# Attention into a soft mixture of experts: routing computed from the transposed attention weights, without building the attention output

## The chip, the cores and the metric

The kernel runs on one core of a Trainium2 chip. The metric is the device time of one execution in microseconds (us). A core has five engines with queues of their own: PE multiplies matrices into PSUM, DVE (VectorE) and ACT (ScalarE) work on rows of elements, POOL (GpSimd) does too but not on PSUM, and SP issues DMAs. PEld is PE's loading of weights, which overlaps its matmuls.

## What is computed

```
k = v = meanpool_4x4(kv).reshape(B, 768, 128) @ w_sr          # B = 4
a = softmax(q @ k.T / sqrt(128))                              # q: (4, 12288, 128)
x = (a @ v).reshape(49152, 128)                               # attention output
logits = x @ phi                                              # 32 slots
d = softmax(logits, over the tokens); slot_input = d.T @ x    # 32 x 128
slot_out = relu(slot_input @ w1[e]) @ w2[e]                   # 8 experts, 4 slots each
c = softmax(logits, over the slots);  out = c @ slot_out      # (49152, 128)
```

The host only transposes and reorders arrays. The output is 25.17 MB.

## The kernel before

The 49152 queries are cut into 96 blocks of 512 (`NB`), 24 to a batch. Every number is split into a high and a low part (`hi`, `lo`), so that a product of two such numbers is three matmuls (hi hi, hi lo, lo hi).

**A block.** ACT and POOL split the queries (`q_hi`, `q_lo`). `qk` makes scores with the 768 keys on partitions (six tiles) and 512 queries along the row. The maximum over the keys then crosses partitions: `rowmax1` (DVE, a reduction that transposes 32x32 squares), `rowmax2`, `rowmax_pe` (a matmul), `rowmax3`, `rowmax4` (a transpose that spreads the maximum again). `sub` (DVE) takes it off the scores, `exp_hi` and `exp_t` (ACT) compute each exponential twice, once rounded to f16 and once in f32, and `plo` (POOL) subtracts the two. `av_hi` and `av_lo` multiply these weights P with V, next to which a column of ones (the sum) and V phi (32 columns) stand: 161 columns, 72 matmuls a block. `av_evac` (ACT) copies the result to `xl`.

**A group** of four blocks then runs `g0` to `g7a`: it divides by the sum, takes the logits into `LL`, keeps a running maximum over tokens, forms the exponentials `D`, and multiplies them with the attention output in `xl` (`g7m`), adding to `acc`.

**Batches and end.** The next batch's keys are summed by DMAs with addition (`kv_acc`, `kv_fold`) while a batch runs, and turned into K and V by `kv_ops`. `k_max`, `k_sub`, `k_exp` prepare the softmax over slots. After the last block come the expert layers (`t_psi` to `t_slo`) and the output: `c_t`, `o_mm`, `o_ev`, `o_dma`.

**What sets the order.** The code is not run in the order it is written. Class `Plan` takes every step with an engine, a cost, a priority and the buffers it takes (`acq`) and uses, simulates the engines with those costs, and emits each engine's instructions in that order; on the chip the engines follow it, waiting on semaphores. Buffers come in rings, e.g. `m` (two PSUM banks for small results), `t` (f32 exponentials). PSUM's other six banks hold scores.

Of the kernel before, what the change touches and what calls it, by code (L numbers as in the profile page):

```python
# [33 lines left out]
class Plan:  # L34
# [22 lines left out]
    def emit(self):  # L57
# [16 lines left out]
        sums = {key: sum(ops[n][0] == "PE" for n in u) for key, u in self.users.items()}  # L74
        summed = {}
# [4 lines left out]
        tops = [None] * self.cap["m"]  # L80
        where = {}
# [6 lines left out]
        def bank(key):  # L88
            found = []
            for b in range(len(banks)):  # L90
                if key[0] == "pq":
                    t = gone(banks[b])
                    beside = banks[b] is not None and banks[b][1][0] == "px" and t == inf
                    if beside:
                        t = summed.get(banks[b], inf)
                    found.append((max(t, gone(tops[b])), not beside, b))
                else:
                    found.append((max(gone(banks[b]), gone(tops[b])), False, b))
            return min(found)

        def acquire(n, now):
            t = 0.0
            for key in ops[n][6]:
                ring = key[0]
                if ring == "m":
                    t = max(t, bank(key[1])[0])
# [28 lines left out]
        while todo:  # L135
# [10 lines left out]
            for key in acq:  # L146
                if key[0] == "m":
                    b = bank(key[1])[2]
                    (tops if key[1][0] == "pq" else banks)[b] = key
                    where[key] = self.bank = b  # L150
                else:
                    rings.setdefault(key[0], []).append(key)
            for key in acq + ops[n][11]:
                left[key] -= 1
                part[key] = max(part.get(key, 0.0), end)
                if eng == "PE":
                    sums[key] -= 1
                    if sums[key] == 0:
                        summed[key] = end + self.LAG
# [13 lines left out]
def attention_then_soft_moe(ctx: ExitStack, tc: tile.TileContext, qT, kv0, kvT, w_sr, w_srT, phi, w1, w2, outT):  # L173
# [10 lines left out]
    GQ = 2048  # L184
# [25 lines left out]
    gp = es.enter_context(tc.tile_pool(name="gp", bufs=1))  # L210
# [12 lines left out]
    make_identity(nc, ident)  # L223

# [27 lines left out]
    nc.vector.memset(acc, 0.0)  # L252

# [3 lines left out]
    VU = {}  # L257
# [31 lines left out]
    QKP = 5  # L289
    SL = 0.5  # L290


    def kv_load(plan_):
        t = kvp.tile([P, KVC, NK], F32, tag="kv", name="kv_0", bufs=2).rearrange("p a b -> p (a b)")
        o = 0
        for h, e0, n in plan_:
            k0, k1 = KS[h]
            w = k1 - k0
            for c in range(e0, e0 + n, 2):
                s = R2 * k0 + c * w  # L300
# [36 lines left out]
    PK_ = {}  # L337

    def kv_k_mm(b, h):
# [5 lines left out]
        pk = PK_[b, h] = mt([P, 512], f"pk_{b}_{h}")  # L345
# [3 lines left out]
    def kv_k_hi(b, h):  # L349
        k0, k1 = KS[h]  # L350
        nc.scalar.activation(kT[b][0][:, k0:k1], PK_[b, h][:, : k1 - k0], AF.Copy, scale=1.0 / R2)

    def kv_k_lo(b, h):
# [3 lines left out]
            out=lo[:, k0:k1], in0=PK_.pop((b, h))[:, : k1 - k0], scalar=1.0 / R2, in1=hi[:, k0:k1].bitcast(F32),  # L357
# [12 lines left out]
    def kv_v_out(b, h):  # L370
        nc.scalar.activation(VU[b][:, 3 * h : 3 * h + 3, :], PK_.pop((b, h, "v")), AF.Copy, scale=1.0 / R2)

    def kv_m(b, k, h):
        if k == 0 and h == 0:
            AM[b] = (
                bp.tile([P, 2, 2], F32, tag="am", name=f"am_{b}", bufs=1),
                bp.tile([P, 2, P], F32, tag="dg", name=f"dg_{b}", bufs=1),
                bp.tile([P, 2], F32, tag="am2", name=f"am2_{b}", bufs=1),
# [3 lines left out]
            out=am[:, k, h : h + 1], in_=VU[b][:, 3 * h : 3 * h + 3, VSRC[k]], axis=XY, op=ALU.max,  # L382
            apply_absolute_value=True,
        )
        if h and k:
            nc.vector.tensor_reduce(out=am2, in_=am, axis=X, op=ALU.max)

    def kv_d(b, k):
        _, dg, am2 = AM[b]
        nc.scalar.activation(dg[:, k, :], ident, AF.Copy, scale=am2[:, k : k + 1])  # L390

    def kv_s_mm(b):
        pa = PK_[b] = mt([P, 512], f"pa_{b}")
        nc.tensor.matmul(
            pa[:, : 2 * P], ones, AM.pop(b)[1].rearrange("p k n -> p (k n)"), start=True, stop=True
        )

    def kv_s_g(b):
        pa = PK_.pop(b)
        pg = pa[:, 2 * P : 2 * P + 2]  # L400
        nc.vector.tensor_reduce(out=pg, in_=pa[:, : 2 * P].rearrange("p (k n) -> p k n", k=2), axis=X, op=ALU.max)
        nc.vector.tensor_scalar_max(pg, pg, 1e-30)
        nc.vector.tensor_single_scalar(pg.bitcast(U32), pg.bitcast(U32), 0x7F800000, op=ALU.bitwise_and)
        g = bp.tile([P, 2], F32, tag="g", name=f"g_{b}")
        nc.vector.tensor_scalar_mul(g, pg, 1.0 / VK)
        inv = bp.tile([P, 2], F32, tag="inv", name=f"inv_{b}")
# [3 lines left out]
    VSRC = (slice(0, C), slice(C, C + NS))  # L410

    def kv_t_hi(b, k):
        inv = VS[b][1]
        if k == 0:
            VU[b] = (
                VU[b],
                bp.tile([P, NT, VW], F16, tag="vhi", name=f"vhi_{b}"),
                bp.tile([P, NT, C + NS], F16, tag="vlo", name=f"vlo_{b}"),
            )
        v, hi, lo = VU[b]  # L420
        src = VSRC[k]
        part = hi[:, :, src.start + 1 : src.stop + 1]
        if b:
            nc.scalar.activation(v[:, :, src], v[:, :, src], AF.Copy, scale=inv[:, k : k + 1])
            nc.scalar.activation(part, v[:, :, src], AF.Copy)
        else:
            nc.scalar.activation(part, v[:, :, src], AF.Copy, scale=inv[:, k : k + 1])

    def kv_t_lo(b, k):
        inv = VS[b][1]  # L430
        v, hi, lo = VU[b]
        src = VSRC[k]
        if b:
            if k == 0:
                nc.gpsimd.memset(hi[:, :, :1], 1.0)
            nc.gpsimd.tensor_tensor(out=lo[:, :, src], in0=v[:, :, src], in1=hi[:, :, src.start + 1 : src.stop + 1], op=ALU.subtract)
            return
        if k == 0:
            nc.vector.memset(hi[:, :, :1], 1.0)
        nc.vector.scalar_tensor_tensor(  # L440
            out=lo[:, :, src], in0=v[:, :, src], scalar=inv[:, k : k + 1], in1=hi[:, :, src.start + 1 : src.stop + 1],
            op0=ALU.mult, op1=ALU.subtract,
        )


    def q_load(g, lo=0, hi=GQ):
# [3 lines left out]
        eng = nc.scalar if hi < GQ else nc.sync  # L450
        eng.dma_start(out=qs[g][:, lo:hi], in_=qT[b, :, o * GQ + lo : o * GQ + hi])
# [801 lines left out]
```

## Time and profile before

| | |
|---|---|
| median of 3 runs | 1116.59 us (1116.41 to 1117.16) |
| span of the profiled execution, first to last instruction | 1112.9 us |
| mean granted PE clock | 0.976 |
| busy PE / PEld / DVE / ACT / POOL | 1044.9 / 893.6 / 984.2 / 829.4 / 870.5 us |
| DMA | 89.15 MB, mean 80 GB/s |

The profile is of one execution, and its own time is given as the span; what lies around the span isn't profiled, and the runs' median is 3.7 us longer. A group row reads: line, engine, operation, output<-input, shapes, count | busy us, mean ns of one | idle time before it and what ended it. A wait row reads: who waited, for whom, us in total, times, longest. A DMA row ends with KB each and us to landing.

### The profile page before, as it was taken

What the parts mean: (1) busy time and instruction counts of PE and PEld (TensorE: products, weight loads), DVE (VectorE), ACT (ScalarE), POOL (GpSimd) and SP (SyncE); (2) the same over time, 40 slices, a digit from 0 to 9 for tenths busy, and PEclk for the clock granted to TensorE, in tenths of its full rate; (3) what the DMA queues carried; (4) which work ended last, traced back from release to release, by engine and by line L of the source; (5) the groups of instructions that cost most, each with busy time, mean ns of one, the idle gap of its engine ahead of it and who ended that gap; (6) DMA issues with size and microseconds to landing.
All of it is one profiled execution on the core that took longest, in us unless ns stands there. A gap on an engine that the chain in (4) does not pass through costs nothing.

```text
span 1112.9 us, 24732 instructions
## 1 busy us (share of the span) xinstructions
PE 1044.9 (94%) x10198; PEld 893.6 (80%) x10198; DVE 984.2 (88%) x1493; ACT 829.4 (75%) x1029; POOL 870.5 (78%) x503
## 2 busy tenths in 40 slices
PE   3699999999999999999999999999999999997885
PEld 2588888888888888888888888888888888886343
DVE  7889889899889989899888988989989988997894
ACT  1677778778777878778777788688778777875563
POOL 0679898798899889789899989789889889873440
PEclk9899999999999999999999999999999999999975
DMA  9218301111136310120145310120110110113498
GB/s 351 108 31 177 70 16 39 39 58 39 39 60 150 82 35 6 39 87 10 39 102 108 82 39 1 39 95 2 39 39 1 39 39 2 39 39 114 145 406 357
DMA packets 17407, 89.15 MB, mean 80 GB/s; under 512 B 1680, under 2 KB 3984, under 8 KB 11152
## 3 DMA queue, kind: packets, MB, share of 16 engines
q1 hardware_dynamic: 13408, 69.47, 17.0%
q0 software_dynamic: 3312, 17.70, 8.4%
q8 instruction: 81, 1.33, 0.5%
q10 hardware_dynamic: 576, 0.41, 0.1%
q14 instruction: 30, 0.25, 0.1%
HBM read 58.87 MB, written 25.17 MB: 76 GB/s over the span
## 4 chain that ended last, share of the span: by engine, by line
PE 61%; ACT 18%; DVE 15%; issue 3%; POOL 2%; DMA 1%; SPq 0%; DVEq 0%; ACTq 0%
PE m L562 10%; PE m L554 10%; PE m L555 9%; ACT phi L528 8%; PE s L476 8%; PE s L478 7%; PE s L477 7%; ACT t L532 7%; DVE t L521 4%; PE m L503 3%; DVE r L483 3%; PE m L707 2%; PE po L1138 2%; DVE o L1147 2%; DVE mb L513 1%
## 5 line engine op out<-in xcount | busy, mean ns | idle before, releaser
L537 POOL TENSOR_TENSOR plo<-t,phi 128x1536 f16<-128x1536 f32 x190 | 598.8, 3156 | 128.1 <-ACT t L532 127.3
L528 ACT ACTIVATE phi<-t,lnk 128x1536 f16<-128x1536 f32 x192 | 301.5, 1570 | 118.9 <-DVE t L521 118.7
L483 DVE TRANSPOSE_TENSOR_REDUCE r<-s 128x32 f32<-128x1024 f32 x288 | 348.6, 1233 | 29.3 <-PE s L478 25.7
L554 PE MATMUL m<-vhi,phi 128*128 128x161 f16 x2280 | 354.7, 234 | 2.8 <-DVE acc L713 1.4
L555 PE MATMUL m<-vlo,phi 128*128 128x160 f16 x2280 | 353.8, 233 | 0.0
L521 DVE TENSOR_TENSOR t<-s,mb 128x1024 f32<-128x1024 f32 (+1 forms) x384 | 342.8, 949 | 9.3
L532 ACT ACTIVATE t<-t,lnk 128x1536 f32<-128x1536 f32 x192 | 301.5, 1570 | 3.6
L476 PE MATMUL s<-qhi,khi 128*128 128x512 f32 x576 | 239.9, 417 | 6.1 <-DVE t L521 5.8
L554 PEld LDWEIGHTS <-phi 128*128 128x128 f16 x2304 | 224.3, 98 | 24.3 <-issue 24.3
L555 PEld LDWEIGHTS <-phi 128*128 128x128 f16 x2304 | 225.1, 98 | 5.4 <-issue 3.5
L562 PE MATMUL m<-vhi,plo 128*128 128x161 f16 x2280 | 226.5, 234 | 0.4 <-POOL plo L537 0.4
L478 PE MATMUL s<-qhi,klo 128*128 128x512 f32 x576 | 226.6, 393 | 0.0
L477 PE MATMUL s<-qlo,khi 128*128 128x512 f32 x576 | 226.1, 392 | 0.0
L562 PEld LDWEIGHTS <-plo 128*128 128x128 f16 x2304 | 178.2, 100 | 1.2 <-POOL plo L537 0.6
L466 POOL TENSOR_TENSOR qlo<-q,qhi 128x512 fp32r<-128x512 f32 x96 | 128.6, 1340 | 26.8 <-ACT qhi L462 26.8
L572 ACT ACTIVATE xl<-m 128x322 f32<-128x322 f32 x189 | 81.4, 430 | 84.5 <-PE m L562 83.8
L476 PEld LDWEIGHTS s<-qhi,khi 128*128 128x128 f32 x576 | 109.2, 190 | 32.6 <-issue 7.5
L478 PEld LDWEIGHTS s<-qhi,klo 128*128 128x128 f32 x576 | 108.8, 189 | 24.7 <-DVE klo L356 0.5
L477 PEld LDWEIGHTS s<-qlo,khi 128*128 128x128 f32 x576 | 109.5, 190 | 18.7 <-issue 0.7
L513 DVE STREAM_TRANSPOSE mb<-m 128x512 f32<-128x512 f32 x96 | 68.3, 711 | 3.3
L462 ACT ACTIVATE qhi<-q 128x512 fp32r<-128x512 f32 x96 | 59.1, 616 | 1.5 <-issue 0.8
L508 DVE TENSOR_REDUCE m<-m 128x16 f32<-128x64 f32 x96 | 21.5, 224 | 40.7 <-PE m L503 40.7
(145 smaller groups left out, 860.1 us busy)
## 6 DMA issues: line engine op xcount, KB each, us to landing
q<-qT SPq DMA_DIRECT2D x23, 1024.0 KB, 4.8
outT<-o SPq DMA_DIRECT2D x21, 1024.0 KB, 5.4
kva<-kvT POOLq DMA_DIRECT2D x9, 1536.0 KB, 11.2
kva<-kvT SPq DMA_DIRECT2D x3, 1536.0 KB, 10.5
kv<-kv SPq DMA_DIRECT2D x8, 512.0 KB, 5.6
w<-w SPq DMA_DIRECT2D x2, 1536.0 KB, 6.4
w<-w SPq DMA_DIRECT2D x4, 768.0 KB, 4.4
outT<-o SPq DMA_DIRECT2D x6, 512.0 KB, 4.7
```

The costliest lines, as they stand in the source:

```text
L466: nc.gpsimd.tensor_tensor(out=lo, in0=q_src(i), in1=hi.bitcast(F32), op=ALU.subtract)
L476: nc.tensor.matmul(s, khi[:, ks], hi, start=True, stop=False)
L477: nc.tensor.matmul(s, khi[:, ks], lo, start=False, stop=False)
L478: nc.tensor.matmul(s, klo[:, ks], hi, start=False, stop=True)
L483: nc.vector.tensor_reduce(out=MX[i][:, 2 * u : 2 * u + 2, :].rearrange("p t b -> p (t b)"), in_=S[i, u].rearrange("p t (b j) -> p (t b) j" ...
L521: nc.vector.tensor_tensor(out=TT_[i, h][:, o : o + n, :], in0=S[i, t // 2][:, u : u + n, :], in1=MX[i].unsqueeze(1).broadcast_to([P, n, BQ ...
L528: nc.scalar.activation(hi, TT_[i, h], AF.Exp, bias=lnk, scale=SCALE)
L532: nc.scalar.activation(t, t, AF.Exp, bias=lnk, scale=SCALE)
L537: eng.tensor_tensor(out=lo, in0=TT_.pop((i, h)), in1=PP[i, h], op=ALU.subtract)
L554: nc.tensor.matmul(px, p, vhi[:, t, :], start=(t == 0), stop=False)
L555: nc.tensor.matmul(px[:, 1:], p, vlo[:, t, :], start=False, stop=False)
L562: nc.tensor.matmul(px, PP[i, t // TH][1][:, t % TH, ks], vhi[:, t, :], start=False, stop=(t == NT - 1))
```

## The change

Scores are made the other way round: queries on partitions (four tiles of 128), the 768 keys along the row. The row's maximum is then a plain reduction (`rowmin`; the keys carry the factor -1/sqrt(128), so that it is a minimum), it enters the exponential as ACT's bias, and ACT adds up the row's sum as it goes (`exp_t`). Each exponential is computed once; ACT copies it to f16 (`t_hi`) and POOL subtracts (`t_lo`).

The attention output is no longer built. The logits are P (V phi): for that P has to stand with keys on partitions. All high tiles and two of six low ones are transposed by DMA (`x_hi`, `x_lo`), the other low ones on PE (`tr`) and copied out by DVE (`tr_out`). `l_mm` then makes the 32 logits of 512 queries, 32 weight columns at a time, in four column strips of PE. Three small transposes turn the 128x128 result back and forth: `l_r` divides by the sum, `colmax` and `d_exp` keep the running maximum and exponentials over tokens, now block by block. The slot inputs are D^T P V: `z_mm` multiplies D with the untransposed P of the block, `z_acc` adds to a 128x768 sum per batch, and only at a batch's end `b_t`, `b_out` and `b_mm` multiply this with V. `f_q` to `f_acc` bring the strips to one maximum at the end.

Around that: the six score banks are two slots of three banks, half a block each; `nh` and `nl` (f16 P) have four buffers, the transposed `pth` and `ptl` two, `t` six of half the size; the q loads move from SP's queue to ACT's and are halved to 512 KB; the sums of keys have one buffer instead of two; three of eight experts' `w1` are loaded early instead of six; the output goes in chunks of three tiles instead of four, through eight buffers instead of four. `Plan` loses its special rule for a bank shared by two results, and its priorities change (`PER`).

```diff
-        nc.tensor.matmul(s, khi[:, ks], hi, start=True, stop=False)
-        nc.tensor.matmul(s, khi[:, ks], lo, start=False, stop=False)
-        nc.tensor.matmul(s, klo[:, ks], hi, start=False, stop=True)
+        cuts = (0, 512, NK) if j % NP == 0 else (0, NK - 512, NK)
+        parts = list(zip(cuts, cuts[1:]))
+        for n, (a, k) in enumerate(((hi, khi), (hi, klo), (lo, khi))):
+            for c0, c1 in parts:
+                nc.tensor.matmul(s[:, c0:c1], a[:, qt], k[:, c0:c1], start=(n == 0), stop=(n == 2))
+
+    def rowmin(i, h):
+        z = (NP * i + h) % NR
+        o = SLOT[i, h] * SW
         nc.vector.tensor_reduce(
+            out=low[:, z, :, 0], in_=sflat[:, o : o + SW].rearrange("p (j k) -> p j k", j=NP), axis=X, op=ALU.min
         )
+        nc.vector.tensor_reduce(out=nm[:, z, :], in_=low[:, z], axis=X, op=ALU.add)
+    def exp_t(i, j):
+        nc.scalar.activation(
+            t, s_of(i, j), AF.Exp, bias=nm[:, z, j % NP : j % NP + 1], scale=-1.0, accum_out=sums[:, i % NR, j, :1]
         )
-        nc.scalar.activation(hi, TT_[i, h], AF.Exp, bias=lnk, scale=SCALE)
-        nc.scalar.activation(t, t, AF.Exp, bias=lnk, scale=SCALE)
+        nc.scalar.activation(nat(NH[i], j), T[i, j].rearrange("p (t k) -> p t k", t=NT), AF.Copy)
+            out=nat(NL[i], j), in0=T.pop((i, j)).rearrange("p (t k) -> p t k", t=NT), in1=nat(NH[i], j), op=ALU.subtract
+    def x_hi(i, h):
+        nc.sync.dma_start_transpose(out=wide(PTH[i], h, 0, NT), in_=run(NH[i], h, 0, NT))
+    def x_lo(i, h):
+        nc.sync.dma_start_transpose(out=wide(PTL[i], h, 0, XT), in_=run(NL[i], h, 0, XT))
...
+        for t in range(XT, NT):
+            for j in range(NP):
+                nc.tensor.transpose(out=b[:, n * P : (n + 1) * P], in_=NL[i][:, h, t, j, :], identity=ident_h)
+        nc.vector.tensor_copy(run(PTL[i], h, XT, NT), b[:, : (NT - XT) * NP * P])
-            nc.tensor.matmul(px, p, vhi[:, t, :], start=(t == 0), stop=False)
-            nc.tensor.matmul(px[:, 1:], p, vlo[:, t, :], start=False, stop=False)
+        for x, u in ((hi, uhi), (hi, ulo), (lo, uhi)):
+            for t in range(NT):
+                for j in range(TB):
+                    nc.tensor.matmul(
+                        pl[j * NS : (j + 1) * NS, :], u[:, t, :], nat(x, j)[:, t, :],
+                        start=(n == 0), stop=(n == 3 * NT - 1),
+                    )
...
+    def z_mm(i, u):
+        for n, (d, x) in enumerate(((0, NH[i]), (1, NH[i]), (0, NL[i]))):
+            for j in range(TB):
+                nc.tensor.matmul(
+                    pz[j * NS : (j + 1) * NS, :], dh[:, d, j * NS : (j + 1) * NS], nat(x, j)[:, u * ht : (u + 1) * ht, :],
+                    start=(n == 0), stop=(n == 2),
+                )
+    def z_acc(i, u):
+            nc.vector.scalar_tensor_tensor(
+                out=z, in0=z, scalar=al[:, i % NRR : i % NRR + 1], in1=pz, op0=ALU.mult, op1=ALU.add
+            )
```

**On PE**, in the middle of the program: `s` and `s6` are score banks, `m0` and `m1` the small banks. Before, the end of a block's scores and the first matmuls of an earlier block's P times V:

```order
L476 MATMUL s_45_2_6464<-qhi_45_6208,khi_1_2403 128x512
L477 MATMUL s_45_2_6464<-qlo_45_6209,khi_1_2403 128x512
L478 MATMUL s_45_2_6464<-qhi_45_6208,klo_1_2404 128x512
L554 LDWEIGHTS phi_43_0_6279
L554 MATMUL m1_115<-vhi_1_3204,phi_43_0_6279 128x161
L555 LDWEIGHTS phi_43_0_6279
L555 MATMUL m1_115<-vlo_1_3205,phi_43_0_6279 128x160
```

Now, the scores of one query tile, a small transpose and the first logit matmul of block 40:

```order
L454 MATMUL s6_120<-khi_1_3432,qhi_44_7951 128x512
L454 MATMUL s6_120<-khi_1_3432,qhi_44_7951 128x256
L454 MATMUL s6_120<-klo_1_3433,qhi_44_7951 128x512
L454 MATMUL s6_120<-klo_1_3433,qhi_44_7951 128x256
L454 MATMUL s6_120<-khi_1_3432,qlo_44_7952 128x512
L454 MATMUL s6_120<-khi_1_3432,qlo_44_7952 128x256
L539 MATMUL m1_119<-ident_84,dt_39_8214 128x128
L527 LDWEIGHTS uhi_1_4456
L527 MATMUL m0_118<-pth_40_7902,uhi_1_4456 32x128
```

A 768-wide row takes two matmuls where there was one of 512, and the 161-wide products with V have given way to 32x128 ones with V phi, four blocks behind the scores.

**On ACT**, a stretch before (`phi` is the f16 exponential, `xl` the copied attention output):

```order
L528 ACTIVATE phi_51_0_7441<-t_51_0_7399,lnk_96 128x1536
L532 ACTIVATE t_51_0_7399<-t_51_0_7399,lnk_96 128x1536
L682 ACTIVATE D_11_7447<-D_11_7447 128x512
L684 ACTIVATE da_11_7449<-da_11_7449 128x32
L528 ACTIVATE phi_51_1_7486<-t_51_1_7438,lnk_96 128x1536
L462 ACTIVATE qhi_54_7507<-q_13_6573 128x512
L532 ACTIVATE t_51_1_7438<-t_51_1_7438,lnk_96 128x1536
L572 ACTIVATE xl_12_7253<-m1_115 128x322
```

and now (`lt` is the logits' copy, `dh` the high part of D):

```order
L467 ACTIVATE t_46_0_8618,sums_110<-s6_120,nm_109 128x768
L467 ACTIVATE t_46_1_8696,sums_110<-s6_120,nm_109 128x768
L535 ACTIVATE lt_42_8702<-m1_119,g_1_4440 128x128
L582 ACTIVATE dh_41_8707<-dr_41_8693 128x128
L418 DMA q_25_8710<-qT 128x1024
L365 ACTIVATE v32_2_8411<-m0_118 128x480
L429 ACTIVATE qhi_48_8735<-q_24_8317 128x512
L383 ACTIVATE dg_2_8506<-ident_84,am2_2_8507 128x128
L482 ACTIVATE nh_45_8762<-t_45_0_8503 128x6x128
L482 ACTIVATE nh_45_8762<-t_45_1_8538 128x6x128
```

The exponentials of a block (46) run a block ahead of its high parts (45 here), and the logits that arrive (42) belong to high parts two blocks further back: those of 43 and 44 lie between.

**On SP**, which held the q loads before:

```order
L755 DMA w1_0_11015<-w1 128x3x1024
L451 DMA q_13_6573<-qT 128x2048
L451 DMA q_14_7157<-qT 128x2048
L451 DMA q_15_7731<-qT 128x2048
L451 DMA q_16_8308<-qT 128x2048
```

and now, two blocks' transposes, each half block a high and a low one:

```order
L502 DMA_TRANSPOSE pth_71_14005<-nh_71_13877 128x12x128
L505 DMA_TRANSPOSE ptl_71_14006<-nl_71_13890 128x4x128
L502 DMA_TRANSPOSE pth_71_14005<-nh_71_13877 128x12x128
L505 DMA_TRANSPOSE ptl_71_14006<-nl_71_13890 128x4x128
L502 DMA_TRANSPOSE pth_72_14162<-nh_72_14037 128x12x128
```

One load a group has become four transposes a block.

More of the change, by code (lines that the diff above doesn't have):

```diff
@@ L86, in gone, with bank @@
             return 0.0 if key is None else freed.get(key, inf)
[L88 to L99, printed above, removed]
+        def bank():
+            return min((gone(key), b) for b, key in enumerate(banks))
         def acquire(n, now):
@@ L575, in bc, with l_sb, t_mm, ll @@
+    def l_sb(i):
+        lt = W["lt", i] = sp.tile([P, P], F32, tag="lt", name=f"lt_{i}")
+        nc.scalar.activation(lt, PK_.pop(("l", i)), AF.Copy, scale=VS[i // BPB][0])
+    def t_mm(key, src):
+        b = PK_[key] = mt()[:, :P]
+        nc.tensor.transpose(out=b, in_=src, identity=ident)
     def bc(a, n):
         return a.unsqueeze(2).broadcast_to([P, a.shape[1], n])
+    def ll(i):
+        return LL[:, i * TB : (i + 1) * TB, :]
+    def l_r(i):
+        nc.vector.tensor_tensor(
+            out=ll(i), in0=PK_.pop(("l1", i)).rearrange("p (j s) -> p j s", j=TB), in1=bc(rr[:, i % NRR], NS), op=ALU.mult
+        )
@@ new lines, in z_acc, with b_t @@
+    def z_acc(i, u):
+        b, ib = divmod(i, BPB)
+        if ib == 0 and u == 0:
+            ZA[b] = sp.tile([P, NK], F32, tag="za", name=f"za_{b}")
+        z = ZA[b][:, u * HK : (u + 1) * HK]
+        pz = PK_.pop(("z", i, u))
+        if ib:
+            nc.vector.scalar_tensor_tensor(
+                out=z, in0=z, scalar=al[:, i % NRR : i % NRR + 1], in1=pz, op0=ALU.mult, op1=ALU.add
+            )
+        else:
+            nc.vector.tensor_copy(z, pz)
+    def b_t(b, u):
+        n = 4 if u == 0 else NT - 4
+        pz = PK_["bt", b, u] = mt()
+        for k in range(n):
+            t = 4 * u + k
+            nc.tensor.transpose(out=pz[:, k * P : (k + 1) * P], in_=ZA[b][:, t * P : (t + 1) * P], identity=ident)
@@ L776, in act @@
         return n / 1200 + 0.08 + 0.093 * aps
-    last = {}
     LAND = 1.46
@@ new lines, in attention_then_soft_moe @@
+        for j in range(TB):
+            h, j2 = divmod(j, NP)
+            p = T0 + 0.25 * PER * j
+            e1 = ops["e", i, j] = op("ACT", act(NK, 1) + ACCT, 0.1, p - 2, [nz[i, h]], lambda i=i, j=j: exp_t(i, j), acq=[("t", (i, j))], use=[("s", (i, h))])
+            e2 = ops["hi", i, j] = op(
+                "ACT", act(NK), 0.1, p + 1, [e1] + ([ops["hi", i, j - 1]] if j else []), lambda i=i, j=j: t_hi(i, j), acq=[] if j else [("nh", i)], use=[("t", (i, j))] + ([("nh", i)] if j else []), raw=0.13
+            )
+            ops["lo", i, j] = op(
+                "DVE" if end else "POOL", 0.9 if end else 1.6, 0.1, p + 2, [e2] + ([ops["lo", i, j - 1]] if j else []), lambda i=i, j=j: t_lo(i, j), acq=[] if j else [("nl", i)],
+                use=[("t", (i, j)), ("nh", i)] + ([("nl", i)] if j else []),
+            )
@@ new lines, in attention_then_soft_moe @@
+        p = T0 + DP * PER
+        u = ("u", b)
+        k = ("m", ("l", i))
+        a = op("PE", 18 * LMM + 0.15, 0.3, p, xs + [ops["u", b]], lambda i=i: l_mm(i), acq=[k], use=[ph, pl, u])
+        a = op("ACT", act(P, 1), 0.1, p, [a], lambda i=i: l_sb(i), acq=[("lt", i)], use=[k])
+        k = ("m", ("l1", i))
+        a = op("PE", 0.13, 0.3, p, [a], lambda i=i: t_mm(("l1", i), W.pop(("lt", i))), acq=[k], use=[("lt", i)])
+        a = ops["L", i] = op("DVE", dve(P) + 0.03, 0.08, p, [a, rc], lambda i=i: l_r(i), use=[k])
@@ new lines, in attention_then_soft_moe @@
+        k = ("m", ("l2", i))
+        a = ops["l2", i] = op("PE", 0.13, 0.3, p, [a], lambda i=i: t_mm(("l2", i), ll(i)), acq=[k])
+        a = op("DVE", 0.3, 0.08, p, [a] + ([nz["nb", i - 1]] if i else []), lambda i=i: colmax(i), use=[k])
+        nz["nb", i] = a
+        de = a = op("ACT", 0.6, 0.1, p, [a], lambda i=i: d_exp(i), acq=[("dt", i)], use=[k])
+        nz["sum"] = op("POOL", 0.2, 0.1, p, [a] + ([nz["sum"]] if i else []), lambda i=i: d_sum(i))
+        k = ("m", ("d", i))
+        a = op("PE", 0.13, 0.3, p, [a], lambda i=i: t_mm(("d", i), W.pop(("dt", i))), acq=[k], use=[("dt", i)])
@@ new lines, in attention_then_soft_moe @@
+        a = op("DVE", dve(P) + 0.03, 0.08, p, [a], lambda i=i: d_r(i), acq=[("dr", i)], use=[k])
+        a = op("ACT", act(P), 0.1, p, [a], lambda i=i: d_hi(i), acq=[("dh", i)], use=[("dr", i)])
+        a = op("POOL", 0.33, 0.1, p, [a], lambda i=i: d_lo(i), use=[("dr", i), ("dh", i)])
+        for v in range(2):
+            k = ("m", ("z", i, v))
+            z = op("PE", 3 * 0.17 + 0.15, 0.3, p, [a], lambda i=i, v=v: z_mm(i, v), acq=[k], use=[("dh", i), nh, nl])
+            za = ("za", b)
+            new = ib == 0 and v == 0
+            prev_acc[v] = op(
+                "DVE", dve(HK) + 0.06, 0.08, p, [z] + ([prev_acc[0] if ib == 0 and v else prev_acc[v]] if i or v else []),
+                lambda i=i, v=v: z_acc(i, v), acq=[za] if new else [], use=[k] + ([] if new else [za]),
+            )
```

886 lines of the change are left out of this document (352 added, 534 removed).

## The prediction

> **What bounds the kernel now.** I read the span and clock first, then busy time in a steady window, then the spacing of blocks, then the chain of waits, and last single groups. One block is 512 queries; there are 96. The window's columns are busy us of PE, PEld, DVE, ACT and POOL, the granted clock, the DMA share and GB/s.
>
> ```profile
> core 0: 1112.9 us, clock 0.976
> core 0: us, PE busy (x) PEld busy (x) DVE busy (x) ACT busy (x) POOL busy (x), PEclk, DMA share, GB/s
> 400.00:600.00 200.00, 197.17 (x1976) 173.28 (x1974) 180.90 (x271) 158.27 (x195) 171.31 (x97) 1.00 0.22 56
> 1090.00:1113.00 23.00, 12.48 (x96) 7.11 (x92) 10.27 (x11) 8.41 (x11) 0.00 (x0) 0.57 0.86 355
> L513 DVE STREAM_TRANSPOSE mb<-m x96: 711/711/714, 30.9 to 1004.6; 128x512 f32<-128x512 f32 x96
> PE 61%; ACT 18%; DVE 15%; issue 3%; POOL 2%; DMA 1%; SPq 0%; DVEq 0%; ACTq 0%
> POOL plo L537 <- ACT t L532: 127.3, 98, 6.9
> ACT phi L528 <- DVE t L521: 118.7, 71, 3.1
> ```
>
> L513 runs once a block: (1004.6 - 30.9)/95 = 10.25 us a block. Of that PE is busy 98.6% (197.17 of 200), so 10.1 us; DVE 9.3, POOL 8.8, ACT 8.1. The chain of waits says the same: 61% of it is PE. ACT and POOL do wait, for each other and for DVE (the two wait lines, about 1.3 us a block each), but PE has no room to let them use it. So the loop is PE-bound at full clock, and 95 x 10.25 = 974 us of the span is loop. The last stretch is output: DMA 86% busy while the engines idle.
>
> **What goes and comes on PE, a block.** Rows that price it, the first four as first and last of seven and of twelve matmuls in a run:
>
> ```profile
> 508.27 0.39 PE L476 MATMUL s<-qhi,khi 128*128 128x512 f32 x1
> 509.63 0.39 PE L476 MATMUL s<-qhi,khi 128*128 128x512 f32 x1
> 506.01 0.23 PE L554 MATMUL m<-vhi,phi 128*128 128x161 f16 x1
> 506.78 0.23 PE L555 MATMUL m<-vlo,phi 128*128 128x160 f16 x1
> L562 PEld LDWEIGHTS <-plo 128*128 128x128 f16 x2304 | 178.2, 100 | 1.2 <-POOL plo L537 0.6 <-issue 0.4
> 1003.82 0.30 PEld L503 LDWEIGHTS m<-rq,sel 128*128 128x128 f32 x2 [0.23 <-DVE rq L495]
> 114.54 1.09 PE L707 MATMUL m<-xl,D 128*32 128x129 f32 x32
> L1058 PE MATMUL ph<-w,sm 128*32 128x512 f32 x32 | 5.0, 782 | 0.3 <-DVE sm L1043 0.3
> L1116 PE MATMUL m<-ident,LL 128*128 128x128 f32 x96 | 18.8, 328 | 3.8 <-POOL LL L747 3.1 <-DVE clo L1126 0.6
> ```
>
> A 512-wide score matmul takes 1.36/6 = 0.227 us, an attention matmul 0.77/11 = 0.070. Removed: 18 x 0.227 = 4.1 us of scores, 48 x 0.070 + 24 x 0.077 (178.2/2304) = 5.2 us of P times V, and the row-maximum and slot matmuls, together the rest of the 10.1. Added:
>
> - Scores: 12 of 512 columns, 2.72 us, and 12 of 256. A 256-wide one is at least half of 0.227; its f32 weight load is the question. Two L503 loads take 0.30 us where one takes 0.19, so they follow each other 0.11 apart: I take 0.115, 1.38 us. If the full 0.19 showed each time it would be 2.28. Scores 4.1 (to 5.0), no gain.
> - 16 f16 transposes of lo tiles at 0.077: 1.24.
> - 72 logit matmuls with 32 weight columns. L707 is the same 128x32 shape, 32 in 1.09 us, 0.034 each; an f32 matmul is two such instructions, an f16 one is one, with half the passes, so 0.017 to 0.034 and 1.2 to 2.45 us. I take 1.5, nearer the low end, since f16 is what runs.
> - 24 slot matmuls of 384 columns on the same tiling. L1058 gives 0.156 for 512 f32 columns; three quarters of it, halved for f16 or not: 0.059 to 0.117, 1.4 to 2.8. I take 1.4.
> - Three small f32 transposes at 0.196 (18.8/96): 0.6. Per-batch work: 0.2.
>
> PE after: 4.1 + 1.24 + 1.5 + 1.4 + 0.6 + 0.2 = 9.0 us, from 8.7 to 12.3.
>
> **ACT.** The four exponentials of 768 read PSUM and take a bias pointer and a sum.
>
> ```profile
> L424 ACT ACTIVATE v<-v,inv 128x768 f32<-128x768 f32 x3 | 2.8, 919 | 0.0
> L425 ACT ACTIVATE vhi<-v 128x768 f16<-128x768 f32 x3 | 2.5, 849 | 0.1
> L462 ACT ACTIVATE qhi<-q 128x512 fp32r<-128x512 f32 x96 | 59.1, 616 | 1.5 <-issue 0.8 <-DMA q<-qT 0.7
> L1104 ACT ACTIVATE shi<-psq,tsum 128x128 fp32r<-128x128 f32 x1 | 0.4, 367 | 0.6 <-PE psq L1099 0.6
> L588 ACT ACTIVATE cq<-quad,cmt 128x4 f32<-128x4 f32 x24 | 6.8, 284 | 1.0 <-DVE cmt L633 1.0
> 500.33 1.56 ACT L528 ACTIVATE phi<-t,lnk 128x1536 f16<-128x1536 f32 x1
> 501.79 0.29 ACT L588 ACTIVATE ru<-r,g 128x16 f32<-128x16 f32 x1
> ```
>
> L424 is a 768-wide operation with a pointer: 0.92. The running sum is in no row; it costs between nothing and another small operation (0.28), and I add 0.1. So exp_t 4 x 1.02, t_hi 4 x 0.85 (L425 is exactly its shape), q_hi 0.62, l_sb 0.37, the two exponentials of d_exp 0.28 + 0.47, d_hi 0.3: 9.5 us of durations. A next operation starts 0.10 before the last has ended (500.33 + 1.56 against 501.79), so 13 of them occupy 8.2. The routing exponentials, per-batch work and the q loads, which now issue from ACT's queue, add about 0.6: 8.8 us (8.4 to 9.5), against 8.1. ACT, which had two us to spare, has none.
>
> **POOL and DVE.**
>
> ```profile
> L537 POOL TENSOR_TENSOR plo<-t,phi 128x1536 f16<-128x1536 f32 x190 | 598.8, 3156 | 128.1 <-ACT t L532 127.3
> L436 POOL TENSOR_TENSOR vlo<-v,vhi 128x768 f16<-128x768 f32 x3 | 4.8, 1591 | 0.0
> L466 POOL TENSOR_TENSOR qlo<-q,qhi 128x512 fp32r<-128x512 f32 x96 | 128.6, 1340 | 26.8 <-ACT qhi L462 26.8
> L747 POOL TENSOR_TENSOR LL<-LL,RM 128x128 f32<-128x128 f32 x1 | 0.4, 402 | 0.0
> L483 DVE TRANSPOSE_TENSOR_REDUCE r<-s 128x32 f32<-128x1024 f32 x288 | 348.6, 1233 | 29.3 <-PE s L478 25.7
> L1147 DVE COPY o<-po 128x1024 f32<-128x1024 f32 x23 | 28.0, 1215 | 5.0 <-PE po L1138 4.9
> L1107 DVE SCALAR_TENSOR_TENSOR slo<-psq,tsum,shi 128x128 fp32r<-128x128 f32 x1 | 0.3, 342 | 0.0
> L695 DVE TENSOR_REDUCE al<-da 128x1 f32<-128x32 f32 x24 | 4.2, 175 | 0.8 <-POOL da L690 0.8
> ```
>
> POOL keeps the big subtraction, cut in four: 4 x 1.59 = 6.36 against 2 x 3.16, plus q_lo 1.34, d_lo 0.4 (L747), d_sum 0.2, and 0.5 for the routing subtraction and DMA issue: 8.8, unchanged; the group arithmetic it loses is made up. On DVE the maximum no longer needs transposes, the cross-partition matmul or the 4 subtractions: two reductions of 1536 (1.5 x 1.23 each as a ceiling, 3.7), z_acc twice 0.6 (between L1107 and L1147 by width), l_r and d_r 0.7, six small ones 1.05, two 1024-wide f16 copies out of PSUM at 0.6 to 1.2 each (half of L1147, or all of it), 0.2 of routing: 8.0 to 9.2, against 9.3. The Trainium skill, VectorE: DVE Perf Modes, "Why PSUM operands drop a tier", lets 16-bit PSUM data run at twice the f32 rate; by that the copies are at the low end and DVE near 8.1, by the row 9.2, and no run here shows it.
>
> **SP and DMA.** Per block 32 tiles of 128x128 f16, 1 MB, now go SBUF to SBUF through DMA transposes, four in a row on SP's queue; no trace of before shows one.
>
> ```profile
> q1 hardware_dynamic: 13408, 69.47, 17.0%
> kva<-kva POOLq DMA_DIRECT2D x3, 768.0 KB, 7.2
> kva<-kva POOLq DMA_DIRECT2D x3, 384.0 KB, 3.9
> L1151 SPq DMA_DIRECT2D outT<-o x27: 332/332/1336, 1045.6 to 1107.1; - x27
> ```
>
> At the plain rate (69.47 MB in 17.0% of 1112.9 us, 367 GB/s) it is 2.9 us. The nearest row is the fold, SBUF to SBUF with an addition: 384 KB more for 3.3 us more, 8.8 us a MB. The addition reads a second operand, so I take half of it, 4.4 us, beside 2.3 us of other traffic (share 0.22). That is hidden under a 9 us block: in the instruction order the high parts and the logits of one block lie two blocks apart, and four nh buffers carry it. If that cover goes, every us over the block length costs 95. Behind SP's waits for these high and low parts stand only each batch's first key load and the expert weights, both issued many blocks or a chain of small steps ahead of use; the q loads have left that queue.
>
> **The sum.** Four engines between 8.0 and 9.2 replace one at 10.1 with the rest below 9.3. The old loop lost 0.15 to waits over its bound; with PE, ACT and POOL within 0.3 of each other a late one has nothing to catch up with, and I allow 0.4, a third of the 1.3 us that POOL alone waits for ACT today: 9.4 us a block. 95 x (9.4 - 10.25) = -81. The end: output is bound by DMA as before (from 1045.6 to the end, 25 MB in 67 us), but about six t_hi are still queued behind the last exponentials, 6 x 0.85 = 5 us (0 to 12; a gain isn't seen, since the rate of the output is the queue's). Head: no change, since the first loads are the same bytes. Span 1112.9 - 81 + 5 = 1037. The runs' median, 1116.6, lies 3.7 above the profiled span, so 1041 us.
>
> **Rivals.** Waits vanish, and the block comes down to its busiest engine, 8.9: 1112.9 - 95 x 1.35 + 8.7 = 993. For it: the old loop ran at 98.6% of its bound. Against: it had one bound, not three.
>
> The lock between ACT and POOL: the t ring has six tiles, so an exponential waits for the low part of six tiles earlier on POOL, which waits for a high part on ACT. Today's two wait lines are this kind; should they keep their 1.2 us, a block is 8.8 + 1.2 = 10.0: 1098.
>
> The transposes bound the loop (slower). If the queue serves them one at a time at the fold's landing times, 2 x (3.9 + 1.7) = 11.2 us, past 10.25; with half of the other traffic in their way 12.4: 1112.9 + 95 x 2.15 + 8.7 = 1326. It decides from 10.25 us a block. Against it: the queue's rows show several transfers in flight. The Trainium skill bears on it from both sides: VectorE: DVE Perf Modes, "The three transpose paths", gives a 128x128 DMA transpose 1309 ns against 390 on TensorE and sends such tiles to TensorE; 32 in series would be an estimated 42 us a block. The same skill's DMA: Bandwidth & Descriptors, "Latency and other measured facts", gives transposes 261 GB/s, by which 1 MB takes an estimated 4.0 us and is hidden. No run here shows either.
>
> PE at its upper end (12.3), with the column tiles not side by side: about 1316. L707 and L1058 speak against it. That the edits do nothing at all needs gains and losses that cancel.
>
> **How the numbers follow.** Forecast 0.50, with 9.1 to 9.7 us a block, 1012 to 1069; waits vanish 0.18; lock 0.17; transposes 0.09; PE 0.03; cancelled 0.03. Slower is the transposes, PE and the worst of the lock (0.03): 0.15; same, within 0.2%, which is about what these timings can tell, 0.03; faster 0.82. The range leaves out the slow rivals (0.13) and the lower third of the fast one (0.06): 985 to 1112.
>
> **What would show it.** rowmin twice a block, spaced 9.4 us a pair; PE busy near 96%, its 128x32 matmuls 0.02 apart; exp_t near 1.0 us and ACT above 90%; transposes landing within a few us. I am wrong if the chain runs through SP or DMA, if ACT's waits for POOL exceed 1 us a block, or if a 256-wide score matmul takes 0.19.

## The result, and the profile after

The changed kernel takes **1664.08 us** (median of 4 runs, 1654.54 to 1670.55) against 1116.88 us before: ratio 1.490, 95% interval 1.485 to 1.495. The forecast was 1041 us, faster. (Where a kernel's times scatter, its median below is of all its runs and its ratio to before only of those near its fastest; x1's ratio alone is of all four.)

After, a steady window, the row minimum (L459, twice a block), the main waits, and the one wait of PE for a transpose. The window's columns are as in the prediction; a wait's are us in total, times and the longest:

```profile
core 0: 1668.8 us, clock 0.823
1000.00:1200.00 200.00, 139.87 (x1830) 104.82 (x1829) 101.04 (x197) 116.53 (x249) 114.71 (x95) 0.86 0.51 97
L459 DVE TENSOR_REDUCE low<-s x192: 1747/1758/1759, 33.2 to 1499.7; 128x2 f32<-128x1536 f32 x192
ACT t L467 <- PE s L454: 282.5, 137, 5.6
PEld s L454 <- ACT t L467: 254.2, 175, 4.2
POOL nl L487 <- ACT nh L482: 246.6, 121, 6.4
DVE low L459 <- ACT t L467: 210.3, 77, 7.3
PE s L454 <- ACT t L467: 204.3, 141, 3.9
ACT t L467 <- DVE low L459: 163.4, 81, 3.9
DVE low L459 <- PE s L454: 154.2, 80, 5.8
PE m L527 <- DMA pth<-nh: 9.5, 1, 9.5
```

A block takes (1499.7 - 33.2)/95.5 = 15.36 us; 9.4 was forecast. No engine is the bound: PE is busy 70% of the window, the others 50 to 58%. PE, DVE and ACT wait for each other in a ring, always over `s`. One of those waits makes no sense as a flow of data: the minimum L459 waits 210 us for the exponential L467, which writes nothing that the minimum reads. PE waits for a transposing transfer once.

Each engine's work on the tile `s` alone (PE, PEld, DVE, ACT) in earlier windows, after and then before:

```profile
200.00:400.00 200.00, 80.38 (x324) 58.45 (x323) 47.44 (x27) 52.68 (x108) 0.86 0.50 100
400.00:600.00 200.00, 78.28 (x318) 55.95 (x317) 47.45 (x27) 51.48 (x105) 0.89 0.69 115
```

```profile
200.00:400.00 200.00, 87.11 (x352) 63.64 (x350) 138.34 (x135) 1.00 0.26 65
```

After, scores, minimum and exponential sum to 80.4 + 47.4 + 52.7 = 180.5 of 200 us. Before, the sum is 87.1 + 138.3 = 225 of 200: they overlapped. By the start and end of each instruction in the trace, no two of these engines work on `s` at once anywhere between 200 and 1000 us. In order of time, PE's, DVE's and ACT's lines on `s` for block 49, up to the first of block 50 (the exponentials at 774.05 and 774.93 are still block 48's):

```profile
771.63 1.76 DVE L459 TENSOR_REDUCE low<-s 128x2 f32<-128x1536 f32 x1 [0.17 <-PE s L454]
...
774.05 0.88 ACT L467 ACTIVATE t<-s,nm 128x768 f32<-128x768 f32 x1
774.93 0.89 ACT L467 ACTIVATE t<-s,nm 128x768 f32<-128x768 f32 x1
...
776.06 0.61 PE L454 MATMUL s<-khi,qhi 128*128 128x512 f32 x2
776.86 0.51 PE L454 MATMUL s<-khi,qlo 128*128 128x512 f32 x2
...
777.49 0.90 ACT L467 ACTIVATE t<-s,nm 128x768 f32<-128x768 f32 x1 [1.32 <-PE s L454]
...
778.53 0.62 PE L454 MATMUL s<-khi,qhi 128*128 128x256 f32 x2 [0.30 <-ACT t L467]
779.33 0.51 PE L454 MATMUL s<-khi,qlo 128*128 128x256 f32 x2
...
779.96 0.90 ACT L467 ACTIVATE t<-s,nm 128x768 f32<-128x768 f32 x1 [0.75 <-PE m L539]
...
780.99 1.76 DVE L459 TENSOR_REDUCE low<-s 128x2 f32<-128x1536 f32 x1 [2.08 <-ACT t L467]
...
782.80 0.80 PE L454 MATMUL s<-khi,qhi 128*128 128x512 f32 x1 [2.40 <-DVE low L459]
```

The scores at 776.06 and 778.53 fill the second slot while the exponentials at 777.49 and 779.96 read the first, so nothing but the tile's name joins them; yet each starts where the other ends. In the program both slots are views of one tile, `s6`, and the order is as if each instruction on any part of that tile waited for all earlier ones of other engines. Before there were three tiles `s0` to `s2`.

### The profile page after: what moved, and what is told of

Its sections match the earlier page's. It is cut to its first block, busy times and chain, and to the rows that moved or that the text cites. A ratio compares the mean times of both kernels' runs of the same rounds, so it can differ in the third digit from the quotient of the medians.

```text
span 1668.8 us, 34763 instructions
## 1 busy us (share of the span) xinstructions
PE 1126.4 (67%) x14062; PEld 823.4 (49%) x14062; DVE 819.7 (49%) x1574; ACT 890.0 (53%) x1890; POOL 882.4 (53%) x748
## 5 line engine op out<-in xcount | busy, mean ns | idle before, releaser
L487 POOL TENSOR_TENSOR nl<-t,nh 128x768 f16<-128x768 f32 x384 | 626.2, 1648 | 247.1 <-ACT nh L482 246.6
L467 ACT ACTIVATE t<-s,nm 128x768 f32<-128x768 f32 x384 | 344.5, 898 | 523.2 <-PE s L454 282.5
L459 DVE TENSOR_REDUCE low<-s 128x2 f32<-128x1536 f32 x192 | 337.4, 1757 | 405.7 <-ACT t L467 210.3
L454 PE MATMUL s<-khi,qhi 128*128 128x512 f32 (+1 forms) x768 | 273.8, 443 | 334.0 <-ACT t L467 204.3
L454 PEld LDWEIGHTS s<-khi,qhi 128*128 128x128 f32 x768 | 138.8, 224 | 420.6 <-ACT t L467 254.2
L482 ACT ACTIVATE nh<-t 128x768 f16<-128x768 f32 x384 | 308.1, 834 | 55.1 <-PE m L596 51.3
L454 PE MATMUL s<-klo,qhi 128*128 128x512 f32 (+1 forms) x768 | 233.7, 391 | 0.0
L454 PE MATMUL s<-khi,qlo 128*128 128x512 f32 (+1 forms) x768 | 233.6, 391 | 0.0
L454 PEld LDWEIGHTS s<-klo,qhi 128*128 128x128 f32 x768 | 160.3, 230 | 22.6
L454 PEld LDWEIGHTS s<-khi,qlo 128*128 128x128 f32 x768 | 160.3, 230 | 22.3
L512 PE MATMUL m<-ident_h,nl 128*128 128x128 f16 x1536 | 135.2, 242 | 33.2 <-DVE dr L575 23.3
L467 ACT ACTIVATION_READ_ACCUMULATOR t<-s,nm 128x1 f32 x384 | 74.9, 195 | 0.0
```

The lines of the kernel that those rows point to most:

```text
L454: nc.tensor.matmul(s[:, c0:c1], a[:, qt], k[:, c0:c1], start=(n == 0), stop=(n == 2))
L459: nc.vector.tensor_reduce(out=low[:, z, :, 0], in_=sflat[:, o : o + SW].rearrange("p (j k) -> p j k", j=NP), axis=X, op=ALU.min)
L467: nc.scalar.activation(t, s_of(i, j), AF.Exp, bias=nm[:, z, j % NP : j % NP + 1], scale=-1.0, accum_out=sums[:, i % NR, j, :1])
L482: nc.scalar.activation(nat(NH[i], j), T[i, j].rearrange("p (t k) -> p t k", t=NT), AF.Copy)
L487: nc.gpsimd.tensor_tensor(out=nat(NL[i], j), in0=T.pop((i, j)).rearrange("p (t k) -> p t k", t=NT), in1=nat(NH[i], j), op=ALU.subtract)
L512: nc.tensor.transpose(out=b[:, n * P : (n + 1) * P], in_=NL[i][:, h, t, j, :], identity=ident_h)
```

## Experiments

Theory A: `s6` as one tile serialises scores, minimum and exponential. Theory B: the transposing transfers and their rings set the period. Theory C: PE is slow because its granted clock fell to 0.82.

**x1: two tiles.** The two slots become two tiles of three banks. Each engine's order in the loop stays; the output stage at the end gets two pairs of banks in place of three.

```
-    s6 = ps.tile([P, 6, 512], F32, tag="s6", name="s6")
+    s3 = [ps.tile([P, 3, 512], F32, tag=f"s{k}", name=f"s{k}") for k in range(2)]
...
-        return sflat[:, o : o + NK]
+        return sflat[SLOT[i, j // NP]][:, o : o + NK]
```

> The one PSUM tile s of six banks becomes two tiles of three banks, one for each pair of query tiles; the order of the loop's instructions stays. Theory A (one tile s is one unit of the semaphores: scores, row minimum and exponential of either half wait for each other, since the rows of tile s fill 177 to 183 of each 200 us and their sum is their union): a block falls from 15.4 us to what its busiest engine needs, 9.2 to 11.5 us by the busy rows of PE, ACT and POOL, so 1100 to 1290 us in all. Theory B (the transposing transfers and the rings of nh and pth set the period): no change, 1640 to 1680 us. Theory C (PE is slow because its granted clock is 0.85): no change either, 1640 to 1680 us.

Measured 1181.37 us median of four (1156.01 to 1196.58; the trace is of the fastest), 1.058 of before (1.054 to 1.063). The minimum's row by line, its wait for the exponential, and a window of the work on `s` (columns as above):

```profile
DVE low L458 <- ACT t L466: 0.8, 2, 0.6
L458 DVE TENSOR_REDUCE low<-s x192: 1726/1757/1761, 36.7 to 1015.4; 128x2 f32<-128x1536 f32 x192
```

```profile
600.00:800.00 200.00, 98.78 (x462) 72.74 (x462) 66.74 (x38) 73.83 (x152) 0.98 0.92 156
```

And four lines in order of time:

```profile
607.19 0.60 PE L454 MATMUL s<-khi,qhi 128*128 128x512 f32 x2
607.60 0.90 ACT L466 ACTIVATE t<-s,nm 128x768 f32<-128x768 f32 x1
607.63 0.51 PE L454 MATMUL s<-klo,qhi 128*128 128x512 f32 x2
607.98 0.52 PE L454 MATMUL s<-khi,qlo 128*128 128x512 f32 x2
```

Now 239 of 200 us; the exponential at 607.60 runs inside the scores of 607.19 to 608.5, and the minimum's wait for the exponential, 210 us before, is down to 0.8. The block is (1015.4 - 36.7)/95.5 = 10.25 us: 5.1 us less from two names for the same banks. The same matmuls run at a clock of 0.98 in this window, with nothing done about the clock, so the low clock was an effect, not the cause. A holds; B and C alone fall.

**x2: no transfers; x3: half the minimum.** Both keep the one tile. x2 drops SP's transposes and lets the logits read untransposed parts; x3 reduces over half of the keys.

```
-        hi, lo = PTH[i], PTL[i]
+        hi, lo = NH[i], NL[i]
```

```
-rearrange("p (j k) -> p j k", j=NP), axis=X, op=ALU.min
+rearrange("p (j k) -> p j k", j=NP)[:, :, : NK // 2], axis=X, op=ALU.min
```

> Leaves out the transposing transfers of SP: the logits read the untransposed high and low parts, so they are not the reference's logits; the order of the four engines stays, tile s is one tile. Theory A: the time stays within 25 us of the changed kernel's 1664 us, since the transfers are no part of the chain through s. Theory B: a block falls to 9 to 11 us, 1050 to 1250 us.

> Each row minimum reads the first 384 of the 768 keys only (half of its computation is left out), about 0.85 us less of DVE 192 times; DVE is busy in 49% of the span. Theory A: the minimum is a link of the one chain through s, so all of it comes back: 150 to 170 us less, 1490 to 1515 us. Theory B and C: DVE has 7 us to spare in a block, so 1645 to 1670 us.

x2 measured 1642.31 us: all transfers together are worth 22 of the 547 us. x3 measured 1483.66, 6 us below its expected range (one run each); its minimum, by line:

```profile
L459 DVE TENSOR_REDUCE low<-s x192: 947/958/959, 34.4 to 1314.6; 128x2 f32<-128x768 f32 x192
```

The minimum lost 192 x 0.80 = 154 us of an engine that idles half of the time, and the kernel lost 180: more than all of it came back (the clock rose from 0.823 to 0.848; whether that is the rest wasn't tried). That is what a link of a single chain would do.

**x6: the same fault put into the kernel before.** Its three score tiles become one, in the same banks.

```
-            S[i, t // 2] = ps.tile([P, 2, BQ], F32, tag=f"s{t // 2}", name=f"s_{i}_{t // 2}")
+            S[i, t // 2] = s6[:, 2 * (t // 2) : 2 * (t // 2) + 2, :]
```

> The kernel before with one edit: its three PSUM tiles of two banks for the scores become one tile of six banks, the same banks in the same order. Theory A: scores on PE (87 of 200 us) and their maxima and differences on DVE (139 of 200 us) sum to 226 of 200 us and can no longer overlap: at least 11.6 us a block and some hops, 12 to 15 us a block, 1280 to 1570 us. Theory B or C: the tiles of this kernel have no transfers behind them and its PE doesn't pause, so 1116 us, within 10.

Measured 1955.91 us, 840 above the kernel before (one run). Work on `s`, PE, PEld and DVE; the transpose that spreads the maximum, once a block (L513 before); and all work in the last stretch:

```profile
200.00:400.00 200.00, 69.90 (x219) 40.55 (x219) 90.76 (x86) 0.00 (x0) 0.94 0.08 26
L518 DVE STREAM_TRANSPOSE mb<-m x96: 711/711/715, 32.1 to 1613.9; 128x512 f32<-128x512 f32 x96
1600.00:1954.00 354.00, 326.65 (x754) 177.62 (x752) 85.99 (x166) 59.23 (x103) 32.91 (x33) 0.16 0.21 80
```

70 + 91 = 161 of 200 where it was 225. The first 94 of the L518 start between 32.1 and 1547.8 us, 16.3 us a block against 10.25: 575 us over 95 blocks, at clocks of 0.93 to 0.96 in most windows. So the fault costs 6 us a block here too. The other 265 us lie at the end, where the granted clock is 0.16 from about 1580 us on. No other trace here shows that, and its cause is open, so these 265 us don't count as the price of the shared tile.

The block itself overshot the expected 12 to 15 us: that took only the durations on `s`, and in the other 39 of 200 us the chain probably passes through the rest of a block, which the fixed order had counted on doing beside it.

**x4: two tiles, no transfers.**

> Two score tiles, and no transposing transfers (logits from untransposed parts). Theory A: not slower than with two tiles alone; what is lower is what the transfers and their rings still cost there. If the split leaves the transfers hidden, within 20 us of it; if the transfers come next, 50 to 200 us lower, down to 1000 to 1100 us. Theory B: the same as without transfers alone, the split adding nothing.

Measured 1132.08 us (one run), 49 below x1's median, its profiled span 24 below, so between the two cases expected. The block is still 10.06 us, so what remained was mostly not the transfers.

**x5, x7: three tiles of one query tile each.** Three two-bank tiles, the minimum per query tile (384 of them), planned anew; x7 is the same without transfers.

```
-    s3 = [ps.tile([P, 3, 512], F32, tag=f"s{k}", name=f"s{k}") for k in range(2)]
+    s2 = [ps.tile([P, 2, 512], F32, tag=f"s{k}", name=f"s{k}") for k in range(3)]
```

> Three PSUM tiles of two banks, each for one query tile (the output stage gets its three pairs of banks back too), the row minimum taken per query tile; the order is planned anew by the same rules. Theory A (what is left above the work of the engines is the waiting for a tile s of three banks as a whole: PE for both exponentials of it, DVE for both scores): by the busy rows of the run with two tiles (PE 172, POOL 171, ACT 167 of 200 us at 10.3 us a block) the work is 8.9 us, so 9.0 to 9.6 us a block, 1030 to 1095 us in all. Rival (the transposing transfers, 80 to 92% of the DMA time in those stretches, or the two m banks hold the loop): it stays at 10.1 to 10.4 us a block, 1135 to 1180 us.

> Three score tiles, and no transposing transfers (logits read the untransposed parts). If the transfers are hidden once the scores run beside each other, within 15 us of the run with three tiles; if they are the next bound, 30 to 100 us lower.

x5: 1129.15 us median of ten, but 1107 to 1147, ratio 0.9996 (0.9964 to 1.0028); it misses its range, and in the trace, of a run of 1137.27 us, a block takes 10.22 us, as the rival had it. x7: 1057.59 (one run), 72 below x5's median, which the expectation gave for transfers that bind. The minimum of x7 by line:

```profile
L451 DVE TENSOR_REDUCE low<-s x384: 926/957/960, 33.4 to 933.2; 128x1 f32<-128x768 f32 x192
```

PE's waits for the transfers in x5:

```profile
PE m L517 <- DMA pth<-nh: 51.0, 7, 24.2
PE m L517 <- DMA ptl<-nl: 20.0, 7, 5.9
```

The longest of them in order of time, on PE, on SP's queue and on POOL's:

```profile
592.59 0.52 PE L517 MATMUL m<-ptl,uhi 128*32 128x128 f16 x24
...
619.28 0.82 PE L517 MATMUL m<-pth,uhi 128*32 128x128 f16 x22 [24.19 <-DMA pth<-nh]
619.80 0.95 PE L517 MATMUL m<-pth,ulo 128*32 128x128 f16 x24
...
589.27 12.63 SPq L495 DMA_TRANSPOSE ptl<-nl  x1
602.07 16.53 SPq L492 DMA_TRANSPOSE pth<-nh  x1
586.11 1.19 POOL L316 DMA_DIRECT2D kva<-kvT  x1
```

Without transfers a block is (933.2 - 33.4)/95.75 = 9.40 us, the forecast's figure; with them, 51 + 20 us of waits in 14 places. The longest comes just behind an accumulating load of the next batch's keys (POOL, 586.11), during which SP's next two transposes take 12.6 and 16.5 us to issue instead of 1.5. That load itself took 33.1 us to land, where the median of the nine is 13.1; which of them held up the other isn't shown.

**x8: more transfers.** `XT = 5` instead of 2.

> Three score tiles, and SP's transfers turn 5 of 6 low tiles in place of 2 of 6 (44 tiles of 128 x 128 a block in place of 32; PE turns 4 in place of 16). The DMA engines were busy 0.8 to 0.9 of the time at 32 tiles in 10.3 us, so 44 tiles take 11 to 12.5 us: if that is a real bound, a block takes 11 us or more, 1180 us or more in all; if those shares are mostly waiting inside the packets, it stays within 25 us of the run with three tiles.

One run, 1109.19 us, inside x5's scatter: the high DMA share, 1.13 to 1.17 here, is not a bound by itself, but more can't be read from it.

**x9, x10, x12: the accumulating loads** left out, halved, quartered.

> Three score tiles with the transfers as they are, but of each next batch's keys only the first quarter is loaded: the three accumulating loads and the two folds of POOL's queue are left out (15 in all, 1.2 us of POOL each). In the run with three tiles the logits' matmuls waited 51 us for transposed high parts and 20 us for low parts, in 14 pieces, the longest 24.2 us, all next to those loads. Theory D (the transposing transfers are hidden, except where they meet those accumulating loads): most of the 70 us come back, 1050 to 1085 us. Rival (the transposing transfers delay the loop all the time): 1105 to 1135 us.

> Three score tiles, and each accumulating load cut into two of half the size, planned one after the other (nothing left out). Theory D: a transposing transfer then waits behind half as much, so part of the 70 us comes back and the runs scatter less: 1070 to 1110 us. Rival (only the total of bytes counts, or POOL's extra 9 us of issuing): 1115 to 1140 us.

> Three score tiles, each accumulating load cut into four (one row of the 4 x 4 window each, 384 KB; the folds as they were). With half loads the logits' matmuls still waited 12 us for transposed high parts and 17 us for low parts, longest 5.0 us. Theory D: another 10 to 25 us come back, less some 8 us for POOL's additional issues: 1085 to 1105 us. Rival (below some size the pieces add as much queueing as they take away): 1100 to 1120 us.

```
-                out=kvs[b], in_=kvT[b - 1, :, c * KVC : (c + 1) * KVC, :], accum_op=ALU.add,
+                out=kvs[b][:, u, :], in_=kvT[b - 1, :, c * KVC + u, :], accum_op=ALU.add,
```

x9: 1069.16 us (one run). x10: 1106.34 us median of ten, 1081.96 to 1117.58, scattered as widely as x5. x12: **1089.98 us** median of five, 1088.40 to 1096.07, ratio to before **0.977 (0.975 to 0.980)**: faster than both kernels, with nothing left out. All of x12 lies below all of x5; x10's lowest is below all of x12, so quarter loads show a lower median and less scatter than half loads, not a lower best. Minimum of x9; then of x12, with its waits:

```profile
L451 DVE TENSOR_REDUCE low<-s x384: 923/957/960, 33.3 to 935.0; 128x1 f32<-128x768 f32 x192
```

```profile
L451 DVE TENSOR_REDUCE low<-s x384: 925/957/960, 34.6 to 958.6; 128x1 f32<-128x768 f32 x192
PE m L517 <- DMA pth<-nh: 9.6, 2, 6.8
PE m L517 <- DMA ptl<-nl: 7.5, 4, 3.3
```

x9, with all transposes in place, has blocks of (935.0 - 33.3)/95.75 = 9.42 us, as without any. So the transposes are hidden except where they meet those loads, and small loads bring the waits from 71 to 17 us, while the two profiled runs differ by 49 us. (x9 also spares POOL some 17 us of issuing, and the order of each of these kernels is planned anew.)

**x11: half loads and `XT = 5`.**

> As with half loads, and SP's transfers turn 5 of 6 low tiles in place of 2 of 6: the run with that alone gave 1109 us against 1129 with 2 of 6, so the DMA time of the packets did not bind. Theory D: 1060 to 1100 us, at or below half loads alone. If the transfers' time does bind once the stalls are smaller: 5 to 40 us above half loads alone.

1131.66 us median of ten (lowest 1111.31; one took 2494.24, why is open), ratio to before 1.0015 (0.9986 to 1.0044), 25 us above half loads alone: theory D's figure missed, on the side that it gave for transfers that bind. PE's waits for transposes are 98 us in its trace, so 44 tiles a block are not hidden, with loads of this size. Why five of six hurt here and not in x8's one run stays open.

## Why the prediction was wrong, by its own steps

- **"Four engines between 8.0 and 9.2 replace one at 10.1."** This is the step that failed. It adds up engines as if scores, minimum and exponential of neighbouring halves could run beside each other, taking the two slots of three banks as two buffers. As one tile they are one buffer: 15.36 - 9.4 = 5.96 us a block, 569 us over 95.5 blocks; the rest of the 623 us is the end, below. The allowance of 0.4 us for waits is where this wait was missing. x1 gives 5.1 of it back by the tile alone, x9 all of it with finer tiles and without the load collisions. That x9 meets the 9.4 so closely is partly luck: PE is busy 184.6 us there between 200 and 400 us, 8.7 us a block where 9.0 was forecast, and the waits are 0.7 rather than 0.4.
- **The terms themselves** were close. The rows after, in the order PE, ACT, DVE, POOL:

```profile
1044.65 1.19 PE m L526 x72
L467 ACT ACTIVATE t<-s,nm 128x768 f32<-128x768 f32 x384 | 344.5, 898 | 523.2 <-PE s L454 282.5
L467 ACT ACTIVATION_READ_ACCUMULATOR t<-s,nm 128x1 f32 x384 | 74.9, 195 | 0.0
L482 ACT ACTIVATE nh<-t 128x768 f16<-128x768 f32 x384 | 308.1, 834 | 55.1 <-PE m L596 51.3
L517 DVE COPY ptl<-m 128x1024 f16<-128x1024 f16 x192 | 131.0, 687 | 88.0 <-PE m L512 83.6
L487 POOL TENSOR_TENSOR nl<-t,nh 128x768 f16<-128x768 f32 x384 | 626.2, 1648 | 247.1 <-ACT nh L482 246.6
pth<-nh SPq DMA_TRANSPOSE x192, 3.9
```

  72 logit matmuls take 1.19 us (1.5 forecast; the row is from x1, at full clock), the running sum is an instruction of its own of 0.195 (0.1), yet at 774.05 and 774.93 above two exponentials with their sums start 0.88 apart (1.02 less an overlap of 0.10 forecast), t_hi 0.834 (0.85), the f16 copy 0.687 (0.6 to 1.2), a low part 1.648 (1.59). The Trainium skill's VectorE: DVE Perf Modes, "Why PSUM operands drop a tier", which put the copy at the low end, agrees with 0.687, against 1.215 for the f32 copy of the same width before. A pair of 512 and 256 score columns starts 0.35 after the last (607.63 to 607.98 in x1's PE rows, 0.342 forecast).
- **Transposes, hidden at 4.4 us a block.** Hidden is right for the loop (x9 against x7: 9.42 and 9.40), and the rival that made them the slow case was not what happened (x2). The size, 4.4, is shown by no run; the DMA share can't give it, since x8's is above 1. Twelve tiles land together in 3.9 us (the row above), so 32 don't cost the 42 us of an estimate tile by tile. The sentence on what stands behind SP's waits was incomplete: it named each batch's first key load, not POOL's accumulating loads, which run beside the transposes; cutting them is worth 39 us between the medians of x5 and x12.
- **ACT and POOL.** POOL waits 247 us for ACT, but mostly since ACT waits for `s`: in x1 it is 81. ACT's wait for POOL stayed at 26 us, far from the lock's 1.2 us a block.
- **The end, +5 us.** From the last minimum to the end: 169 us after, against 108 before (1112.9 - 1004.6); the output stage's products and evictions share `s6` too, and the granted clock is 0.50 from 1580 us on. With three tiles 1135.5 - 1013.3 = 122, x12 128, so 14 to 20 rather than 5 stay, probably as the blocks still in flight drain through the long chain of small steps.
- **"I am wrong if".** None of its signs came, as far as the rows show: they watched the rivals that I had, and the ring over `s` was none of them. The signs for the forecast failed instead: the minima's spacing, PE at 70% of the window rather than 96, ACT at 58 rather than above 90. It could be read ahead of time: the change turns three tiles into one, and in the changed program's listing with its waits, 139 of the 192 minima wait for ACT (60 in x1), for example

```
L459 TENSOR_REDUCE low_107<-s6_120 128x2 [waits PE_49,Activation_49]
```

Open: how much of x5's gain over x1 is the finer tile, how much the new order and the third pair of banks at the output, which came with it (52 us between the medians, 1181 and 1129). That the two small banks `m` hold x1 was a guess and wasn't tried.

## What to carry to other kernels

Count buffers by what the semaphores see, not by bytes: where two slots were slices of one PSUM tile, engines that worked on different slots still took turns, and a free rename into separate tiles was worth 483 us here (1664 to 1181, the medians). When no engine is near its limit, sum the work of all engines on each shared tile and look at it in order of time: 180 and 161 of 200 us without any overlap were a queue of one here, 225 and 239 with separate tiles were not. Small transfers that a block waits for should not meet large loads; cutting those loads in four took 39 us off the median.

## What was new about the hardware

PE's granted clock was lower where PE made long pauses: 0.86 in the window above where PE was busy 70%, and 0.98 at 85% in x1, with the same instructions. The busy share alone doesn't set it: x6 has 0.94 at 74%. By the matmuls' rows between 200 and 600 us, the changed kernel's PE pauses 123 us in all, 19 times for over 2 us, at clocks of 0.86 and 0.89; x6's pauses 108 us, never for over 2 us, at 0.94. x1's window, all work:

```profile
600.00:800.00 200.00, 169.09 (x2684) 129.82 (x2673) 146.15 (x283) 165.67 (x355) 170.27 (x142) 0.98 0.92 156
```

In x5, after a pause of 24.2 us, 24 logit matmuls took 0.95 us instead of 0.52. The Trainium skill says in TensorE: Matmul & The Clock Gate, "Part 1: The HAM clock gate (the "warmup" mystery)", that the array's clock is halved unless it was lately busy; the 0.95 against 0.52 agrees. The same 14062 matmuls kept PE busy 1126.4 us in the changed kernel and 951.9 in x1, so serialising costs twice: the waits it adds are also paid in slower matmuls.

A DMA transpose of 12 tiles holds SP for 1.49 us (median) and lands after 3.9; beside one accumulating load, at 849.5 us, issuing took up to 17.7 us and landing 37.8 (its row by line, and its landing):

```profile
L502 SPq DMA_TRANSPOSE pth<-nh x192: 1288/1487/17698, 45.1 to 1518.9; - x192
DMA to landing us min/median/max: 3.6/3.9/37.8
```
